# First products directly behind the first gathered rows, and a wider planning margin for routing steps in the sparse groups

## The chip, the cores and the metric

One core of a Trainium2 chip runs the whole program. The metric is the time of one execution in device microseconds (us). Other times in this document are us from the start of the profiled span unless marked ns.

## The reference

Three stages follow each other. The first is attention over a window of 64 positions (4 batches, 8 heads, 576 positions, 64 values a head). The second routes each of the 2304 resulting rows of 512 values to one of 8 experts and applies that expert's two-layer network. The third is one dense two-layer network with a squared ReLU. The routing is greedy over all scores in descending order with room for 288 rows an expert, which is what makes it a search:

```python
logits = x @ w_gate
order = np.argsort(-logits.flatten())
for idx in order:
    tok, e = idx // E, idx % E
    if assigned[tok] >= 0 or counts[e] >= cap: continue   # cap = N // E = 288
    assigned[tok] = e; counts[e] += 1
for e in range(E):
    out[assigned == e] = np.maximum(x[assigned == e] @ w1[e], 0) @ w2[e]
h = np.maximum(out @ w_in, 0)
return h * h @ w_out
```

## The kernel before

**Stages.** `attention` computes the rows and writes them to memory (`xs`) and their routing scores to `L`. Then `FFN.run` goes through the list `ORDER`: sparse groups `M` (one expert each, 288 rows) and dense groups `G` (768 rows each, the third stage): M0 M1 M2 G0 M3 M4 M5 G1 M6 M7 G2. A dense group starts as soon as the experts behind it have delivered its rows.

**The search.** An expert is filled before the next one can be chosen, so `Routing.phase(i)` finds which expert fills next and the score at which it is full. It does six rounds. Each compares all scores against a grid of thresholds on VectorE (line 392; 354 or 382 in the first round), counts on TensorE with 18 small matmuls (line 399, "count"), turns the counts into flags on VectorE (line 426), sums the flags on TensorE (line 432, "sum") and narrows the grid. A prefix sum follows (lines 469 and 470, "prefix"); it is then known which expert it is (`esi`, line 463). `Routing.slots` turns the places into row numbers with 18 more matmuls (line 516, "slots"). All of them share one bank of PSUM.

**From the search to a group.** `FFN.dispatch(i)` issues three gathers of 96 rows on GpSimd's queue (line 791), transposes them on TensorE (line 804, 12 transposes), and splits them into a high part on ScalarE (`xhi`, line 807) and the rest on VectorE (`xlo`, line 809). Each weight tile is split in the same way: the high part on ScalarE (`whi`, line 680), the rest in two halves on VectorE or GpSimd (`wlo`, line 693). A product of two such numbers takes three matmuls: high by high, high by rest, rest by high.

**A sparse group.** `FFN.M(i)` does 96 products for the first layer (8 column blocks, 4 row blocks, 3 passes; line 870) and 96 for the second (line 912), with ReLU and a split in between (lines 891 and 893). The first group, whose weights and rows arrive last, does part of its first layer differently: six column blocks are begun, two at a time, with the two passes that need only the weights' high parts (line 881, 48 products in three waves of 16), and the third pass follows later.

**What sets the order.** The program is straight-line: each engine executes its instructions in the order in which the Python code issues them. That order is made by a planner, `Clock`, which books a duration for each instruction and engine. `clk.pe` is its time; a product of a sparse group moves it by `MM_M` = 121 ns in `tick`. The search, the dispatch and the weight splits are generators. Each yields the planner's time at which it wants to go on. `route_step` resumes search and dispatch; `item_step` resumes the weight splits. `wait_until` and `run_until` take both kinds of steps until a time or a condition is reached; `idle` only moves the planner's time to the next one that something waits for and issues no step. The next weight tile of a sparse group is begun only when both rests of the tile before it have been issued. The time at which a TensorE step of the search may be issued is the planned end of the VectorE work before it plus a margin:

```python
    def after_dve(self):
        return self.dve+60+self.margin
```

The shared bank is given free at the same moment. `G` sets the margin to `MARGIN_G` at its start and to `MARGIN_M` at its end, and `run` sets `MARGIN_M` once the first search is over. Before a sparse group starts, `M` waits (in planned time) until its rows are gathered and split, and `need` waits until the weight tiles asked for are split too. `GATE` lets search 3 and later ones begin only inside dense groups.

The searches are numbered by the expert whose rows they find: search 0 has nothing beside it, searches 1 and 2 run beside the first two sparse groups.

Of the kernel before, what the change touches and what calls it, by code (L numbers as in the profile page):

```python
# [541 lines left out]
GATE_M=2  # L542
GATE=[[0, 1, 3], [0, 5, 4], [0, 9, 5], [1, 1, 6], [1, 7, 7]]
LO_EARLY=2000
MARGIN_M=100
MARGIN_G=100
MM_M=121
GATHER_0=1700
# [5 lines left out]
class FFN:  # L554
# [300 lines left out]
    def M(self, i):  # L855
        nc=self.nc
        n0=self.first["M",i]
        self.run_until(lambda: i in self.x)
        self.wait_until(self.x[i]["at"])
        self.low=n0  # L860
        self.need(n0+3,("hi",) if i==0 else ("hi","lo"))
        self.allowed=n0+8
        self.warm=None
        x=self.x.pop(i)
        h={}; ps={}; hat={}
        def mm(f, passes, c):
            for kk in range(4):
                for a,b in passes:
                    if c: self.tick(MM_M)
                    nc.tensor.matmul(ps[f][:,:CAP],self.w[n0+kk][a][:,f*128:(f+1)*128],x[b][:,kk],start=c==0,stop=c==11)  # L870
                    c+=1

        head=6 if i==0 else 0
        for f in range(0,head,2):

            for g in (f,f+1): ps[g]=self.ps.tile([128,512],F32,name="acc",bufs=6)
            for part in range(2):
                for g in (f,f+1):
                    for kk in range(4):
                        if f==0 and part==1: self.wait_until(x["lat"][kk])  # L880
                        nc.tensor.matmul(ps[g][:,:CAP],self.w[n0+kk]["hi"][:,g*128:(g+1)*128],x[("hi","lo")[part]][:,kk],start=part==0 and kk==0,stop=False)
                        self.tick(MM_M)
        if head: self.need(n0+3)
        for f in range(8):
            if f<head: mm(f,PASSES[2:],8)
            else:
                ps[f]=self.ps.tile([128,512],F32,name="acc",bufs=6)
                mm(f,PASSES,0)
            h[f]=self.htile()
            hi,lo,p=h[f]["hi"][:,:CAP],h[f]["lo"][:,:CAP],ps.pop(f)  # L890
            nc.scalar.activation(hi,p[:,:CAP],AF.Relu); t=self.clk.aop(CAP)
            def low(lo=lo,hi=hi,p=p,t=t,f=f):
                nc.vector.scalar_tensor_tensor(lo,p[:,:CAP],0.0,hi.bitcast(F32),op0=OP.max,op1=OP.subtract)
                hat[f]=self.clk.op(CAP,t,0)+60
            self.defer(t,low)
            self.tick(MM_M)
        self.l1done=i
        self.low=n0+4
        self.need(n0+7)
        self.allowed=n0+12  # L900
        s0=i*CAP
        for d in range(4):
            p=self.ps.tile([128,512],F32,name="acc",bufs=6)
            c=0

            for k,(a,b) in [(k,ab) for ab in (PASSES[0],PASSES[2],PASSES[1]) for k in range(8)] if d==0 else [(k,ab) for k in range(8) for ab in PASSES]:
                if d==0 and b=="lo":
                    self.run_until(lambda: k in hat)
                    self.wait_until(hat[k])
                o=(k%2)*512+d*128  # L910
                if c: self.tick(MM_M)
                nc.tensor.matmul(p[:,:CAP],self.w[n0+4+k//2][a][:,o:o+128],h[k][b][:,:CAP],start=c==0,stop=c==23)  # L912
                c+=1
            g0=s0//HN
            parts=[]
            for g in (g0,g0+1):
                a,b=max(s0,g*HN),min(s0+CAP,(g+1)*HN)
                if a>=b: continue
                y=self.ytile(g)
                sl=slice(a-g*HN,b-g*HN)  # L920
                parts.append((y["hi"][:,d,sl],y["lo"][:,d,sl],p[:,a-s0:b-s0],b-a))
            for yh,yl,src,n in parts:
                nc.scalar.copy(yh,src); t=self.clk.aop(n)
            def low(parts=parts,t=t):
                for yh,yl,src,n in parts:
                    nc.vector.tensor_tensor(out=yl,in0=src,in1=yh.bitcast(F32),op=OP.subtract); self.clk.op(n,t,0)
            self.defer(t,low)
            self.tick(MM_M)


    def G(self, g):
# [75 lines left out]
        self.inG=False  # L1007
        self.clk.margin=MARGIN_M
    def run(self):
        self.gens=[self.route.phase(0,self.o[0])]  # L1010
        self.run_until(lambda: not self.gens)
        self.clk.margin=MARGIN_M
        self.gens=[self.dispatch(0),self.router()]
        for kind,i in ORDER:
            getattr(self,kind)(i)
# [46 lines left out]
```

## Time and profile before

| what | us |
|---|---|
| time, median of 3 runs | 827.7 (825.53 to 828.62) |
| the profiled execution | 828.17 |
| its span | 826.5 |
| TensorE matmuls busy (PE) | 774.8, 94% of the span |
| weight loads busy (PEld) | 702.5, 85% |
| VectorE busy (DVE) | 474.4, 57% |
| ScalarE busy (ACT) | 400.5, 48% |
| GpSimd busy (POOL) | 263.9, 32% |

The profile cuts the span into 40 slices of 20.7 us. In tenths, TensorE's busy share and the clock that was granted to it are

```profile
PE   8899966899998989899999999999999999999995
PEclk9899976899998999999999999999999999999998
```

The attention stage takes the first five to six slices; search 0 stands alone behind it, and the first sparse group begins within the seventh slice. A line of the profile reads: engine, line of the kernel, operation, out<-in, tile shapes, how many. "L" is a line of the kernel printed above. PE is a matmul, PEld its weight load; SPq and POOLq are the queues on which transfers are issued. Products overlap in the pipeline, so the duration of one is longer than its spacing to the next.

### The profile page before, as it was taken

How to read it: one execution, taken by the hardware profiler on the slowest of the kernel's cores; microseconds unless marked ns; L12 is line 12 of the kernel's file. 1: busy time of each engine (PE TensorE's matmuls, PEld its weight loads, DVE VectorE, ACT ScalarE, POOL GpSimd, SP SyncE). 2: the span in 40 equal slices, each digit the busy share in tenths (PEclk: the TensorE clock that was granted, in tenths of full speed). 3: DMA queues.
4: the chain of work that ended last, by engine and by line, in shares of the span. 5: the costliest groups of instructions: out<-in, count | busy, mean ns of one | idle time of the engine just before them, and what ended most of it. 6: DMA issues, size and time to landing. Idle time of an engine off the chain costs nothing.

```text
span 826.5 us, 16334 instructions
## 1 busy us (share of the span) xinstructions
PE 774.8 (94%) x6389; PEld 702.5 (85%) x6389; DVE 474.4 (57%) x1400; ACT 400.5 (48%) x777; POOL 263.9 (32%) x240
## 2 busy tenths in 40 slices
PE   8899966899998989899999999999999999999995
PEld 7788855788997778688899998888999999999995
DVE  5687878787688999977564546542215452222111
ACT  4687722333654554643355444445445455545432
POOL 4121102333633344422254641212215462221103
PEclk9899976899998999999999999999999999999998
DMA  9999715352655565532255541223114442120001
GB/s 168 178 185 196 158 43 173 127 167 104 210 203 202 174 208 195 182 112 81 89 176 197 159 149 52 81 75 108 52 51 172 162 158 98 51 73 31 1 1 76
DMA packets 93132, 104.89 MB, mean 127 GB/s; under 512 B 59776, under 2 KB 67968, under 8 KB 93056
## 3 DMA queue, kind: packets, MB, share of 16 engines
q1 hardware_dynamic: 89984, 94.41, 39.5%
q0 software_dynamic: 3072, 9.45, 3.5%
q8 instruction: 50, 0.82, 0.4%
q14 instruction: 26, 0.21, 0.1%
HBM read 86.01 MB, written 17.84 MB: 126 GB/s over the span
## 4 chain that ended last, share of the span: by engine, by line
PE 39%; issue 15%; POOL 2%; DVE 1%; ACT 0%; POOLq 0%
PE acc L985 11%; PE l L966 11%; PE acc L870 8%; PE acc L912 7%; POOL wlo L693 2%; PE rt L399 1%; POOL out_dram L955 1%; PE acc L804 0%; PE rt L966 0%; PE rt L516 0%; PE rt L432 0%; PE rt L804 0%; DVE wt L663 0%; DVE M L456 0%; DVE hlo L975 0%
## 5 line engine op out<-in xcount | busy, mean ns | idle before, releaser
L693 POOL TENSOR_TENSOR wlo<-wr,whi 128x512 fp32r<-128x512 f32 x90 | 142.3, 1599 | 265.9 <-ACT whi L680 238.8
L975 DVE TENSOR_TENSOR hlo<-h,hhi 128x384 fp32r<-128x384 f32 x96 | 56.2, 586 | 159.0 <-ACT hhi L973 159.0
L970 ACT ACTIVATE r<-l 128x384 f32<-128x384 f32 x93 | 45.6, 490 | 191.6 <-PE l L966 191.5
L966 PE MATMUL l<-yhi,wlo 128*128 128x384 f32 x372 | 127.5, 343 | 0.0
L966 PE MATMUL l<-ylo,whi 128*128 128x384 f32 x372 | 126.6, 340 | 0.0
L966 PE MATMUL l<-yhi,whi 128*128 128x384 f32 x372 | 126.3, 340 | 0.0
L985 PE MATMUL acc<-whi,hlo 128*128 128x512 f32 x288 | 115.5, 401 | 3.8 <-DVE hlo L975 3.8
L985 PE MATMUL acc<-wlo,hhi 128*128 128x512 f32 x288 | 115.0, 399 | 0.0
L985 PE MATMUL acc<-whi,hhi 128*128 128x512 f32 x288 | 113.8, 395 | 0.0
L680 ACT CAST whi<-wr 128x1024 fp32r<-128x1024 f32 x96 | 99.8, 1050 | 28.2 <-DVE G L382 20.2
L693 DVE TENSOR_TENSOR wlo<-wr,whi 128x512 fp32r<-128x512 f32 x102 | 89.5, 883 | 22.7 <-ACT whi L680 22.5
L966 PEld LDWEIGHTS l<-yhi,whi 128*128 128x128 f32 x372 | 70.4, 189 | 4.4 <-ACT hhi L973 0.4
L870 PE MATMUL acc<-xhi,wlo 128*128 128x288 f32 x256 | 73.6, 300 | 0.0
L966 PEld LDWEIGHTS l<-ylo,whi 128*128 128x128 f32 x372 | 70.3, 189 | 3.6
L693 POOL TENSOR_TENSOR wlo<-wt,whi 128x512 fp32r<-128x512 f32 x32 | 46.8, 1485 | 81.1 <-ACT whi L680 81.1
L966 PEld LDWEIGHTS l<-yhi,wlo 128*128 128x128 f32 x372 | 70.2, 189 | 1.3 <-issue 1.1
L870 PE MATMUL acc<-xlo,whi 128*128 128x288 f32 x232 | 69.3, 299 | 0.0
L870 PE MATMUL acc<-xhi,whi 128*128 128x288 f32 x232 | 69.3, 299 | 0.0
L985 PEld LDWEIGHTS acc<-whi,hlo 128*128 128x128 f32 x288 | 54.4, 189 | 16.5 <-DVE hlo L975 4.2
L912 PE MATMUL acc<-hhi,whi 128*128 128x288 f32 x256 | 67.1, 296 | 0.0
L912 PE MATMUL acc<-hlo,whi 128*128 128x288 f32 x256 | 66.7, 296 | 0.0
L912 PE MATMUL acc<-hhi,wlo 128*128 128x288 f32 x256 | 66.4, 295 | 0.0
(198 smaller groups left out, 1473.4 us busy)
## 6 DMA issues: line engine op xcount, KB each, us to landing
wr<-in_moe_w_dram SPq DMA_DIRECT2D x32, 1024.0 KB, 5.3
wr<-conv SPq DMA_DIRECT2D x16, 1024.0 KB, 4.9
wr<-in_moe_w_in_dram SPq DMA_DIRECT2D x16, 512.0 KB, 4.5
wr<-in_moe_w_out_dram SPq DMA_DIRECT2D x16, 512.0 KB, 5.3
conv<-wt SPq DMA_DIRECT2D x16, 512.0 KB, 3.1
xs<-X SPq DMA_DIRECT2D x12, 384.0 KB, 4.6
kn<-in_k_dram SPq DMA_DIRECT2D x20, 192.0 KB, 5.1
qn<-in_q_dram SPq DMA_DIRECT2D x20, 192.0 KB, 5.4
```

Of the source, the lines that this page charges most:

```text
L399: nc.tensor.matmul(cnt[:,0:8],G[:,c],oh[:,c],start=c==0,stop=c==W-1)
L680: nc.scalar.copy(hi,src)
L693: (nc.gpsimd if p else nc.vector).tensor_tensor(out=lo[:,s],in0=src[:,s],in1=hi[:,s].bitcast(F32),op=OP.subtract)
L870: nc.tensor.matmul(ps[f][:,:CAP],self.w[n0+kk][a][:,f*128:(f+1)*128],x[b][:,kk],start=c==0,stop=c==11)
L912: nc.tensor.matmul(p[:,:CAP],self.w[n0+4+k//2][a][:,o:o+128],h[k][b][:,:CAP],start=c==0,stop=c==23)
L955: st=nc.gpsimd.indirect_dma_start(out=self.out,out_offset=bass.IndirectOffsetOnAxis(ap=idt[:,t:t+1],axis=0),in_=ot,in_offset=None)
L966: nc.tensor.matmul(p[:,:HN],self.w[n0+f][a][:,kk*128:(kk+1)*128],y[half][b][:,kk],start=c==0,stop=c==11)
L970: nc.scalar.activation(r,p[:,:HN],AF.Relu); at=self.clk.aop(HN)
L975: nc.vector.tensor_tensor(out=h["lo"],in0=h2,in1=h["hi"].bitcast(F32),op=OP.subtract); self.clk.op(HN,t,0)
L985: nc.tensor.matmul(acc[3*half+t],h[b][:,t*128:(t+1)*128],w[a][:,512:1024],start=f==0 and c==0,stop=f==15 and c==2)
```

## The change

`MARGIN_M` goes from 100 to 400 ns; `MARGIN_G` stays at 100. In `M`, the first group no longer waits in planned time for the split of its rows and for the high parts of its first four weight tiles. It only goes on with the weight splits until the four high copies have been issued. The other groups do what they did (`need` has both parts as its default).

```diff
-MARGIN_M=100
+MARGIN_M=400
 MARGIN_G=100
...
         self.run_until(lambda: i in self.x)
-        self.wait_until(self.x[i]["at"])
         self.low=n0
-        self.need(n0+3,("hi",) if i==0 else ("hi","lo"))
+        if i==0:
+
+            while not all(k in self.w for k in range(n0,n0+4)):
+                if not self.item_step(): self.idle()
+        else:
+            self.wait_until(self.x[i]["at"])
+            self.need(n0+3)
         self.allowed=n0+8
```

## Rows read from the trace of the kernel before

**Rows 1.** Stages: busy us of each engine, granted clock, DMA share, GB/s.

```profile
core 0: us, PE busy (x) PEld busy (x) DVE busy (x) ACT busy (x) POOL busy (x), PEclk, DMA share, GB/s
...
412.00:490.00 78.00, 78.00 (x600) 77.96 (x599) 42.43 (x75) 38.78 (x70) 43.15 (x32) 1.00 0.54 181
```

**Rows 2.** Chain that ended last, pieces in order of time: start, us, what.

```profile
412.07 12.79 PE acc L870 x96
```

**Rows 3.** Timeline of TensorE, 137 to 147: start, us, instruction, idle before, releaser.

```profile
137.72 0.60 PE L399 MATMUL rt<-oh,G 128*128 128x8 bf16 x18
...
141.33 0.63 PE L399 MATMUL rt<-oh,G 128*128 128x8 bf16 x18 [1.35 <-DVE G L392]
141.82 0.59 PE L881 MATMUL acc<-xhi,whi 128*128 128x288 f32 x1
...
144.83 2.12 PE L881 MATMUL acc<-xlo,whi 128*128 128x288 f32 x8
```

**Rows 4.** Timeline of ScalarE, 137 to 141.

```profile
137.72 0.40 ACT L807 CAST xhi<-acc 128x288 fp32r<-128x288 f32 x1 [3.08 <-issue]
...
138.88 2.02 ACT L680 CAST whi<-wr 128x1024 fp32r<-128x1024 f32 x2
```

**Rows 5.** Timelines of GpSimd and TensorE, 155 to 167.

```profile
155.39 4.97 POOL L693 TENSOR_TENSOR wlo<-wr,whi 128x512 fp32r<-128x512 f32 x4 [5.79 <-ACT whi L680]
...
159.22 0.19 PE L469 MATMUL rt<-M,tri 128*128 128x36 bf16 x1 [2.19 <-DVE esi L463]
160.50 0.18 PE L470 MATMUL rt<-cum,on 128*128 128x36 bf16 x1 [1.08 <-DVE cum L464]
...
165.71 1.22 PE L912 MATMUL acc<-hhi,whi 128*128 128x288 f32 x8
```

**Rows 6.** Short stages where the granted clock (PEclk) falls or returns.

```profile
141.50:142.00 0.50, 0.50 (x19) 0.50 (x15) 0.47 (x3) 0.00 (x0) 0.00 (x0) 0.50 1.36 66
...
148.00:148.50 0.50, 0.50 (x5) 0.50 (x5) 0.00 (x0) 0.00 (x0) 0.50 (x2) 0.70 1.07 410
...
162.00:163.00 1.00, 1.00 (x6) 1.00 (x5) 0.95 (x7) 0.00 (x0) 0.00 (x0) 0.50 0.84 319
...
165.00:166.00 1.00, 1.00 (x8) 1.00 (x8) 1.00 (x4) 0.09 (x1) 0.00 (x0) 0.82 1.02 422
```

**Rows 7.** Timelines of SyncE's queue and TensorE, 160 to 184.

```profile
160.31 1.07 SPq L629 DMA_DIRECT2D wr<-in_moe_w_dram  x2
...
169.39 0.61 PE L516 MATMUL rt<-Bv,A__170 128*128 128x6 f16 x18
...
180.14 0.16 PE L432 MATMUL rt<-ok,on 32*128 32x1 bf16 x1 [0.55 <-DVE ok L426]
...
183.76 0.29 PE L870 MATMUL acc<-xhi,whi 128*128 128x288 f32 x1
```

**Rows 8.** Timelines of TensorE and GpSimd, 187 to 216, and the gathers' landing there.

```profile
187.05 0.61 PE L399 MATMUL rt<-oh,G 128*128 128x8 bf16 x18 [0.30 <-DVE G L392]
...
195.68 0.61 PE L399 MATMUL rt<-oh,G 128*128 128x8 bf16 x18
...
203.59 0.61 PE L516 MATMUL rt<-Bv,A__170 128*128 128x6 f16 x18
...
207.54 1.33 POOL L791 DMA_INDIRECT xg<-xs,idx  x1 [0.30 <-issue]
DMA to landing us min/median/max: 3.5/3.9/4.6
212.04 1.16 PE L804 MATMUL acc<-identf,xg 96*128 96x96 f32 x12
...
215.56 0.29 PE L870 MATMUL acc<-xhi,whi 128*128 128x288 f32 x1
```

**Rows 9.** Waits of TensorE, 137 to 260: us in total, times, longest.

```profile
PE acc L985 <- DVE hlo L975: 3.8, 1, 3.8
PE rt L432 <- DVE ok L426: 3.6, 4, 1.5
```

## The prediction before the run

> **What bounds the kernel now.** I read the profile from the outside in: the page's slices, the stage table, then the order of TensorE's instructions inside the first three sparse groups, because both edits act there and nowhere else. In a late sparse group TensorE is busy all the time [rows 1], and 96 products follow each other in 12.79 us [rows 2], that is 0.133 us each; 192 of them, one group, cost 25.6 us. The first group does not look like that. Its first product starts at 141.82 and the second group's first one at 183.76 [rows 3, 7]: 41.9 us for 25.6 us of products. The 16.3 us between are what the change can touch, and they are search steps that stand in TensorE's order, waits for VectorE behind such steps, and a low clock. A search after the third does not stand in a sparse group: the counting matmuls of searches 3 to 7 lie in the dense groups, where the margin stays 100. So the wider margin acts on searches 1 and 2 alone.
>
> **Part 1, the first products.** Before, the planner walked on until the split of x and the four high copies of w1 were done by its clock, and put into TensorE's order what came due meanwhile: one count, one sum and a second count stand between the transposes and the first product [rows 3]. All three wait for VectorE. Now the first product comes as soon as the fourth high copy has been issued, and the loop that waits for it takes no search step. On the chip the first product then needs the first x copy, which ends at 137.72+0.40 = 138.1, and the third and fourth weight copies, which end at 139.9 and 140.9 [rows 4]. So the fourth product starts at 140.9 at the latest, and the first wave of 16 ends twelve products later: at 142.5 if they take 0.133 us, at 144.1 at the slow spacing of the present wave, 2.12/8 = 0.265 us [rows 3]. It ends at 146.95 now. Gain: 2.9 to 4.4 us.
>
> The clock decides between the two. TensorE had nearly nothing to do from 138.3 to 141.3; the granted clock was at half (1.2 GHz of 2.4) from 141.5 and came back in the slice at 148.0 [rows 6]. With products from 138.1 on the empty stretch is shorter; that it then stays up is possible, not certain, and I keep both ends.
>
> Up to product 48 the new order holds the two counts and two sums that stood ahead: 32 products, 4.3 us, and 1.1 us for the four steps, plus up to 1 us of low clock. Up to product 96 (the start of the second layer, 165.71 now [rows 5]) come 6.4 us and 1.2 us for search steps, plus 0 to 2 us of waits. What goes there is the stall of 2.19+1.08 us behind the prefix matmul and the half clock that followed it at 162 [rows 5, 6]. So the second layer starts between 155.5 and 160.1. It takes 96 products, 12.8 us, one to two more search steps, 1 us, and 0 to 1 us of waits: group 0 ends between 169.3 and 175. I take 170.5, near the early end, because the waits shrink by part 2 as well.
>
> **What is late next.** The search. Its steps have lost the head start of three steps. The counts between steps in the present order (16, 7, 10, 6, 13, 6, 11 products, then 55 to the slot matmul, which stands behind product 124 [rows 7]) average ten, so the three steps plus the sixteen products of the wave put the rest some 40 products later. Part 2 adds to that.
>
> **Part 2, the margin.** A search step goes into the order 300 ns later by the planner's clock, which counts 121 ns a product: 2.5 products more in front of each, 0.33 us of TensorE at 0.133 us. A search has 14 such steps (six counts, six sums, prefix, slots). The good side is bounded by the waits in this stretch: TensorE waited 3.6 us in four times for the flag of a count [rows 9], and the stalls above. A margin takes at most 0.33 us of each, some 2 us over both searches, already in the ranges above. The bad side: search 1 now has twelve steps behind the first product, 30 products. With the 40 from part 1 its slot matmul goes from behind product 124 to about 192: the end of the group. What stood behind it there (the first counts of search 2 and the transposes of the next x, some 5 us of the present second layer) leaves the group, and that is half of the group's gain: moved, not saved. No DMA moves by itself, but two queues follow the search: SyncE asks for expert 1's weights once the prefix step has named it (160.31 now [rows 7]), and GpSimd issues the gathers behind the slots. The weights come some 2 to 4 us later and had over 20 us to the group that reads them; for the gathers there is no such room.
>
> This rule speaks against the margin: the Trainium skill, SBUF — State Buffer, section "SBUF: two separate sides", says that VectorE (with two SBUF inputs or in a two-port mode) and GpSimd hold a shared port in turn for whole instructions. The trace bears that out: GpSimd ran four subtractions of weights, 4.97 us, over the prefix stall [rows 5]. By the rule a step that meets a subtraction waits over a microsecond, so 300 ns hides little; taking no relief from the margin would put the sum about 1 us up.
>
> **From slots to the next group.** From the slot matmul to the next group's first product runs a chain that no order shortens: index, three gathers, transposes, split. For group 2: slots 203.59, third gather issued 207.54, 3.9 us to landing (211.4), transposes 1.2 us [rows 8], first x copy 0.4 [rows 4]: 213.0, or 9.4 us after the slots; 9.0 to 10.1 by the spread of the landings. For group 1 this chain is hidden now: 169.39+9.4 = 178.8, and the group starts at 183.76 [rows 7]. With the slots at the end of group 0 it is bare: group 1 starts at 170.5+9.4 = 179.9, 3.9 us earlier than now, after some 9 us in which TensorE has only three short steps of search 2. So the clock falls there. For its price the nearest row is the fall at 162, behind 3.3 us of idling: low to about 165.4 [rows 6], 3.4 us, of which nearly half is lost, 1.5. The longer low stretch, 141.5 to 148.2, would cost 3. I take 1.5.
>
> Search 2: count, sum, count fit into the gap, the next sum (now 10.75 us after the slots [rows 7]) does not. So at the start of group 1 search 2 is a round behind. A round takes (195.68-187.05)/2 = 4.3 us [rows 8], less six products, 3.5 us. From the group's start to slots 2 it was 203.59-183.76 = 19.8; now 19.8+3.5 + ten steps at 0.33 (3.3) - 0.6 of shorter waits + 1.5 of clock = 27.5: slots 2 at 207.4, 3.8 later. The chain of 9.4 us then gives group 2 at 216.8 against 215.56 [rows 8], because its slack of 2.5 us (213.0 to 215.56) is used up first. Group 1's products end by about 212, so TensorE idles again and group 2 too begins at the low clock: another 1.5.
>
> Sum: +1.2 +1.5 = 2.7 us later at the end of group 2. The dense group behind it does not give it back: its first stall, 3.8 us [rows 9], stands behind weights that load after expert 2's, and these follow search 2. The profiled execution took 828.17 (its span 826.5, 1.7 around it), 0.5 above the median of 827.7: 830.9 beside it, 830.4 beside the median.
>
> [...]
>
> **Rivals.**
> *Slower: the search is the bound of both groups.* The point from which it decides is slots 2 at 206.1: beyond it every microsecond is the program's. For it: some 30 more products in each search and two bare gather chains. If group 0 ends at 174, at the late end, and each low clock costs 2, then group 1 starts at 183.4, slots 2 come at 211.4, group 2 at 220.8: +5.2+2 = 7, 835. Against it: a step that comes late waits for nothing, and in the gap search 2 runs undisturbed.
> *Faster: the search keeps up.* If VectorE, not the margin, sets the spacing of the steps, search 2 does not grow by 3.3; with group 0 over at 169.3 and the clock up, group 1 starts at 178.5, slots 2 come at 201.2 and group 2 starts at 210.6: -5, 823. For it: sums and counts wait up to 1.5 us for VectorE now [rows 9], time that a later place uses. Against it: 30 products a search are more than those waits.
> *The first products gain nothing*, because the fourth weight copy holds them to 140.9 and the clock falls as now. Then group 0 loses its stalls only, its slots stay inside it, and the margin makes slots 2 later by 3 to 5: 829 to 833.
>
> **How the numbers follow.** Forecast 0.42, slower 0.29, faster 0.19, no gain in front 0.10. A measurement of this kernel cannot tell less than 0.5%, 4.1 us, from no change: the borders are 823.6 and 831.8. The forecast's own range, 826 to 833, lies mostly inside; a seventh of it and half of the last case go to slower, and a few hundredths of each to faster. So faster 0.18, same 0.46, slower 0.36. The range over all cases is 822.5 (the faster case, a little past it) to 836.5 (the slower one).
>
> **What would show it.** Right: first product near 138.1 and the first wave over by 144; slots of search 1 behind product 180 to 192; an idle stretch of 5 us or more ahead of the second group and one of 3 us or more ahead of the third, each followed by half clock; the start of group 2 between 214 and 219. Wrong: the slots of search 1 well inside group 0, or group 1 and 2 starting with no gap: then the first 3 to 5 us stay won and the time is near 823.

## The result and the profile after

The changed kernel takes 835.27 us (median of 4 runs, 834.28 to 840.61) against 826.62 us (825.03 to 828.62) for the kernel before: a ratio of 1.0101, 95% interval 1.0071 to 1.0131. It is about 1% slower. The profiled execution took 835.46, 7.3 more than that of before. In `M` and behind it the changed file has five more lines: L870 is now L875, L881 is L886, L912 is L917, L966, L975 and L985 are L971, L980 and L990.

The head of the page says that no engine has much more to do; the spans differ, the busy times hardly:

```profile
span 833.4 us, 16329 instructions
PE 775.7 (93%) x6387; PEld 704.0 (84%) x6387; DVE 471.0 (57%) x1404; ACT 399.9 (48%) x777; POOL 258.1 (31%) x236
PE   8899957969998997999999999999999999999996
PEclk9999967969999999999999999999999999999998
```

TensorE is busy 0.9 us longer in a span that is 6.9 us longer: what came is mostly idle time. The medians are 8.65 us apart; the lengths below are those of the two profiled executions, 7.3 apart.

**The start of group 0**, TensorE's timeline (columns as in [rows 3]):

```profile
137.34 1.00 PE L886 MATMUL acc<-xhi,whi 128*128 128x288 f32 x3 [0.18 <-ACT xhi L807]
139.18 1.38 PE L886 MATMUL acc<-xhi,whi 128*128 128x288 f32 x5 [0.84 <-ACT whi L680]
140.36 2.12 PE L886 MATMUL acc<-xlo,whi 128*128 128x288 f32 x8
142.28 0.44 PE L886 MATMUL acc<-xhi,whi 128*128 128x288 f32 x1
```

Against [rows 3], the first product waits for the x copy and for nothing of the search, starts 4.5 us earlier, and the second wave begins at 142.28. The spacing of the third line, 2.12 us for eight, is still that of half clock; the mean granted clock was 1.00 from 137 to 139 and 0.56 from 139 to 142.3.

**From group 0 to group 1.** TensorE again; the rows answer to the prefix of [rows 5] and to the slots and first product of [rows 7]:

```profile
164.92 0.19 PE L469 MATMUL rt<-M,tri 128*128 128x36 bf16 x1
...
170.87 0.60 PE L516 MATMUL rt<-Bv,A__170 128*128 128x6 f16 x18
...
180.09 0.16 PE L432 MATMUL rt<-ok,on 32*128 32x1 bf16 x1 [2.85 <-DVE ok L426]
180.18 0.90 PE L804 MATMUL acc<-identf,xg 96*128 96x96 f32 x4
182.28 1.54 PE L804 MATMUL acc<-identf,xg 96*128 96x96 f32 x8 [1.19 <-DMA xg<-xs,idx]
183.61 0.67 PE L399 MATMUL rt<-oh,G 128*128 128x8 bf16 x18
184.14 0.59 PE L875 MATMUL acc<-xhi,whi 128*128 128x288 f32 x1
```

The prefix waits no longer. The slots of search 1 now stand behind the last product of group 0, and between 171.5 and 184.1 TensorE has only steps of search 2 and transposes, and is busy for 4.5 of these 12.6 us. Group 0 begins 4.5 us earlier, group 1 0.4 us later: nothing of the new start is left.

**From group 1 to group 2**, where [rows 8] had the slots at 203.59 and the transposes at 212.04, inside group 1:

```profile
207.59 0.61 PE L516 MATMUL rt<-Bv,A__170 128*128 128x6 f16 x18
...
215.37 0.29 PE L917 MATMUL acc<-hhi,wlo 128*128 128x288 f32 x1
215.50 1.15 PE L804 MATMUL acc<-identf,xg 96*128 96x96 f32 x12
216.90 0.40 PE L875 MATMUL acc<-xhi,whi 128*128 128x288 f32 x1 [0.24 <-ACT xhi L807]
218.70 0.40 PE L875 MATMUL acc<-xlo,whi 128*128 128x288 f32 x1 [1.40 <-DVE xlo L809]
```

The transposes now follow the last product of group 1; what they and the split take, and a wait of 1.40 us, lie bare. The first dense group begins at 244.1 instead of 241.0.

**The first dense group** ends (first product of M3) at 418.8 instead of 411.9: it is 174.7 us long and was 170.9. TensorE's waits from 240 to 420 (us in total, times, longest), first after, then before:

```profile
PE rt L432 <- DVE ok L426: 9.4, 6, 4.5
...
PE rt L399 <- DVE oh L385: 2.0, 1, 2.0
PE acc L990 <- DVE hlo L980: 1.0, 1, 1.0
...
```

```profile
PE acc L985 <- DVE hlo L975: 3.8, 1, 3.8
PE rt L432 <- DVE ok L426: 3.0, 4, 1.4
...
```

The stall of [rows 9], 3.8 us, has shrunk to 1.0. In its place the waits for the flags of the searches in this group (3 to 5) grew from 3.0 to 9.4; the longest, 4.5 at 332.28, stands behind the slots of search 3 (318.75), in the first round of search 4. The whole lists, of six rows each, add up to 15.5 and 13.5. The clock is the other part; the whole dense group and stages of it (columns as in [rows 1]), first after, then before:

```profile
244.10:418.80 174.70, 159.15 (x1090) 135.43 (x1089) 142.29 (x331) 83.74 (x136) 57.05 (x46) 0.96 0.45 153
244.10:270.00 25.90, 22.51 (x125) 19.88 (x124) 25.68 (x44) 15.63 (x26) 10.20 (x8) 0.93 0.58 198
270.00:300.00 30.00, 26.79 (x185) 22.28 (x184) 28.03 (x52) 14.63 (x23) 9.02 (x6) 0.94 0.52 181
300.00:340.00 40.00, 35.46 (x216) 31.13 (x215) 34.10 (x71) 19.10 (x31) 14.25 (x11) 0.91 0.57 189
```

```profile
241.00:411.90 170.90, 157.26 (x1090) 133.23 (x1089) 143.57 (x328) 84.10 (x136) 61.35 (x47) 0.98 0.45 154
241.00:270.00 29.00, 25.25 (x133) 22.53 (x132) 26.01 (x44) 16.48 (x27) 10.44 (x8) 0.88 0.52 177
270.00:300.00 30.00, 27.98 (x214) 23.32 (x213) 29.30 (x54) 15.53 (x24) 12.64 (x8) 1.00 0.61 207
300.00:340.00 40.00, 34.24 (x217) 28.88 (x215) 38.14 (x80) 21.47 (x34) 16.34 (x12) 1.00 0.52 176
```

VectorE is busy for 85 to 99% of these stages in both. Before, the clock fell once, behind the one stall; after, in three stages. Stage length times what the clock lacks of 1 is at most 3.5 us before and 7.2 after (25.9 x 0.07 + 30 x 0.06 + 40 x 0.09). The first rows say what came of it: with the same number of matmuls TensorE was busy 1.9 us longer (159.15 against 157.26), and so 1.9 of the 3.8 us are matmuls that took longer and 1.9 are idle time. From M3 on the changed kernel stays 6.5 to 6.9 us behind, to the end: 3.1 came in the sparse groups and 3.8 in the dense one.

### The profile page after: what moved, and what is told of

The parts are those of the page before. It is cut to its first block, busy times and chain, and to the rows that moved or that the text cites. A ratio compares the mean times of both kernels' runs of the same rounds, so it can differ in the third digit from the quotient of the medians.

```text
span 833.4 us, 16329 instructions
## 1 busy us (share of the span) xinstructions
PE 775.7 (93%) x6387; PEld 704.0 (84%) x6387; DVE 471.0 (57%) x1404; ACT 399.9 (48%) x777; POOL 258.1 (31%) x236
## 4 chain that ended last, share of the span: by engine, by line
PE 38%; issue 15%; POOL 3%; DVE 2%; DMA 1%; ACT 1%; POOLq 0%; SPq 0%; DVEq 0%; ACTq 0%
PE acc L990 11%; PE l L971 11%; PE acc L875 8%; PE acc L917 6%; POOL wlo L693 2%; PE rt L399 1%; DMA wr<-in_moe_w_out_dram 1%; POOL out_dram L960 1%; DMA wr<-conv 1%; PE acc L804 0%; DVE wt L663 0%; DVE wa L661 0%; DVE wt L665 0%; ACT wa L656 0%; PE rt L971 0%
## 5 line engine op out<-in xcount | busy, mean ns | idle before, releaser
L693 POOL TENSOR_TENSOR wlo<-wr,whi 128x512 fp32r<-128x512 f32 x86 | 138.1, 1621 | 266.4 <-ACT whi L680 243.1
L980 DVE TENSOR_TENSOR hlo<-h,hhi 128x384 fp32r<-128x384 f32 x96 | 55.6, 580 | 160.6 <-ACT hhi L978 160.3
L975 ACT ACTIVATE r<-l 128x384 f32<-128x384 f32 x93 | 45.6, 490 | 205.7 <-PE l L971 205.7
L971 PE MATMUL l<-yhi,wlo 128*128 128x384 f32 x372 | 128.0, 344 | 0.0
L971 PE MATMUL l<-ylo,whi 128*128 128x384 f32 x372 | 127.4, 342 | 0.0
L971 PE MATMUL l<-yhi,whi 128*128 128x384 f32 x372 | 127.3, 342 | 0.0
L990 PE MATMUL acc<-whi,hlo 128*128 128x512 f32 x288 | 116.1, 403 | 1.0 <-DVE hlo L980 1.0
L990 PE MATMUL acc<-wlo,hhi 128*128 128x512 f32 x288 | 115.4, 401 | 0.0
L680 ACT CAST whi<-wr 128x1024 fp32r<-128x1024 f32 x96 | 99.8, 1050 | 32.4 <-DMA wr<-in_moe_w_dram 28.2
L990 PE MATMUL acc<-whi,hhi 128*128 128x512 f32 x288 | 114.2, 396 | 0.0
L971 PEld LDWEIGHTS l<-ylo,whi 128*128 128x128 f32 x372 | 70.6, 190 | 6.2 <-issue 2.5
L971 PEld LDWEIGHTS l<-yhi,whi 128*128 128x128 f32 x372 | 70.7, 190 | 3.6
L875 PE MATMUL acc<-xhi,wlo 128*128 128x288 f32 x256 | 72.9, 298 | 0.0
L971 PEld LDWEIGHTS l<-yhi,wlo 128*128 128x128 f32 x372 | 70.8, 190 | 0.2
L990 PEld LDWEIGHTS acc<-whi,hlo 128*128 128x128 f32 x288 | 54.7, 190 | 19.2 <-issue 6.9
L875 PE MATMUL acc<-xlo,whi 128*128 128x288 f32 x232 | 69.4, 299 | 1.4 <-DVE xlo L809 1.4
L875 PE MATMUL acc<-xhi,whi 128*128 128x288 f32 x232 | 70.0, 302 | 0.2 <-ACT xhi L807 0.2
L917 PE MATMUL acc<-hhi,whi 128*128 128x288 f32 x256 | 67.5, 297 | 0.0
L917 PE MATMUL acc<-hhi,wlo 128*128 128x288 f32 x256 | 66.7, 295 | 0.0
L917 PE MATMUL acc<-hlo,whi 128*128 128x288 f32 x256 | 66.1, 295 | 0.0
```

The lines of the kernel that those rows point to most:

```text
L680: nc.scalar.copy(hi,src)
L693: (nc.gpsimd if p else nc.vector).tensor_tensor(out=lo[:,s],in0=src[:,s],in1=hi[:,s].bitcast(F32),op=OP.subtract)
L971: nc.tensor.matmul(p[:,:HN],self.w[n0+f][a][:,kk*128:(kk+1)*128],y[half][b][:,kk],start=c==0,stop=c==11)
L975: nc.scalar.activation(r,p[:,:HN],AF.Relu); at=self.clk.aop(HN)
L980: nc.vector.tensor_tensor(out=h["lo"],in0=h2,in1=h["hi"].bitcast(F32),op=OP.subtract); self.clk.op(HN,t,0)
L990: nc.tensor.matmul(acc[3*half+t],h[b][:,t*128:(t+1)*128],w[a][:,512:1024],start=f==0 and c==0,stop=f==15 and c==2)
```

## The experiments

Each was timed beside the kernel before on the same chip; they ran on three chips, so that ratios are compared and not times. Lengths are from each one's profile, in us: from the slot matmul of search 0 to that of search 1, on to that of search 2, on to group 2's first product, on to the dense group, and the length of that.

| kernel | ratio (95%) | slots 0 to 1 | 1 to 2 | to group 2 | to dense | dense |
|---|---|---|---|---|---|---|
| before | 1 | 40.4 | 34.2 | 12.0 | 25.4 | 170.9 |
| after | 1.0101 (1.0071 to 1.0131) | 42.8 | 36.7 | 9.3 | 27.2 | 174.7 |
| margin alone | 1.0095 (1.0064 to 1.0125) | 41.5 | 36.0 | 9.2 | 27.3 | 174.4 |
| new start alone | 0.9992 (0.9970 to 1.0014) | 38.4 | 34.9 | 11.7 | 25.4 | 168.4 |
| new start, search in it | 1.0043 (1.0023 to 1.0064) | 41.2 | 34.9 | 11.0 | 26.0 | 173.2 |
| after, search 3 a step later | 1.0020 (1.0003 to 1.0037) | 42.8 | 36.2 | 9.3 | 26.7 | 167.7 |
| margin 400 in search 1 | 1.0015 (0.9996 to 1.0033) | 40.9 | 34.4 | 12.8 | 25.4 | 170.2 |
| margin 400 in search 2 | 1.0067 (1.0041 to 1.0093) | 40.5 | 37.3 | 8.1 | 28.2 | 173.0 |
| new start, search 3 a step later | 0.9940 (0.9918 to 0.9962) | 39.3 | 34.7 | 11.7 | 25.4 | 164.4 |
| before, search 3 a step later | 0.9957 (0.9933 to 0.9981) | 42.4 | 34.2 | 12.0 | 25.4 | 165.3 |
| after, weights behind gathers | 1.0106 (1.0049 to 1.0164) | 43.9 | 36.6 | 9.3 | 25.9 | 171.9 |

The last row but one has before's order up to the dense group, so 40.4 against 42.4 is what one profile scatters; the ratios carry the verdicts.

**The margin alone.**

```diff
-MARGIN_M=100
+MARGIN_M=400
```

> The margin alone (400 ns, the old start). In its instruction order the slots of search 1 stand behind product 170 of the first group (124 before, 192 in the changed kernel) and those of search 2 behind product 138 of the second (114 before, 137 changed). Theory A (the margin makes the searches the bound; the new start is nearly free): group 0 ends near 180 to 183, the second group starts 3 to 5 us later than before, the third 4 to 7 later; time +5 to +8 us over before, 832 to 835. Rival S (the start alone costs, because the search loses the steps that stood ahead of the first product; the margin's steps are paid by shorter waits): within +-2.5 us of before, 824 to 829. Theory B (the first dense group's time hangs on how search steps and conversions happen to interleave): the start of that group is where A says, and its length differs from before (170.9) by 2 us or more in either direction.

Measured 835.01, 1.0095. The margin makes the whole loss.

**The new start alone** (`MARGIN_M` stays 100, `M` as in the changed kernel).

> The new start alone, with the margin at 100 ns as before. The slots of search 1 stand behind product 152, 40 short of the first group's end, those of search 2 behind product 116 of the second group. Theory A: the first product near 138, group 0 over 5 to 8 us earlier, the second group within 2 us of where it was because the gathers behind slots 1 bound it; time -2 to +2 us against before, 825 to 829. Rival S: the second and third group 3 us or more later, time +4 to +7, 831 to 834. Theory B as above: the dense group's length, not its start, carries most of any difference.

Measured 826.93, 0.9992: no difference that can be told. The first product is early here too (139.3), and search 1 ends some 2 us earlier by its profile, which is no more than one profile scatters; in the median nothing arrives.

**The new start with search steps in its loop**, margin 100, to give back the head start.

```diff
-                if not self.item_step(): self.idle()
+                x0=self.item_step(); x1=self.route_step()
+                if not (x0 or x1): self.idle()
```

> The new start with one line more: the loop that waits for the fourth high copy also takes search steps, margin 100 ns. The slots of search 1 stand behind product 126 again (124 before). If what the new start loses is the search's head start (A and S agree on that), this keeps the earlier first product and loses nothing: group 0 ends 2 to 4 us earlier than before, the second group follows it by 0 to 2 us, time -1 to -4 us, 823 to 826. If the early products only move work (the search is the bound whatever stands ahead of it), the third group starts where it did and the time is within 1.5 us of before.

A miss: 831.26, 1.0043. The steps taken in the loop stand ahead of the first product again (it starts at 143.2), slots 1 to 2 is that of the other margin-100 kernels, and the dense group, whose order of instructions comes out a third way, is 173.2 long.

**The changed kernel with search 3 let into the dense group one step later.** The sparse part is untouched.

```diff
-GATE=[[0, 1, 3], [0, 5, 4], [0, 9, 5], [1, 1, 6], [1, 7, 7]]
+GATE=[[0, 2, 3], [0, 5, 4], [0, 9, 5], [1, 1, 6], [1, 7, 7]]
```

> The changed kernel with search 3 let in one step later in the first dense group (step 2 instead of 1); nothing before that group changes, and the sparse groups' order is the same up to its start. Theory A (lateness passes through): 835 +-1.5, the dense group as long as in the changed kernel (174.7 us). Theory B (the interleaving sets it): the dense group's length moves by 2 us or more, and the time with it, to 830 to 833 or to 837 to 840, with its start unmoved.

Measured 828.89, 1.0020, under the 830 to 833 that the second reading named. Against the changed kernel's 1.0101 some 0.8% are gone, with the dense group again beginning at 243.8 and now 167.7 long. Whether this takes back what the margin cost, or would speed up any of the kernels, only the last pair below can tell. Its waits there:

```profile
PE rt L399 <- DVE oh L385: 4.1, 1, 4.1
PE rt L432 <- DVE ok L426: 2.6, 3, 1.1
...
```

The flags cost 2.6 instead of 9.4; one wait of 4.1 stands at the start of the search.

**The margin in search 1 only, and in search 2 only**, each on the kernel before (`i==1`, then `i==2`).

```diff
+            if not self.inG: self.clk.margin=400 if i==1 else MARGIN_M
             yield from self.route.phase(i,self.o[i])
```

> The old start; the margin is 400 ns for search 1 and 100 for search 2. The order of every engine inside the first dense group is then instruction for instruction that of the kernel before, while the slots of search 1 go from behind product 124 to behind product 168. Theory C (the loss is made by search 2: it is the one whose end no group hides, and its end relative to the third group decides the dense group's order): within +-2 us of before, 825.5 to 829.5; dense group 168 to 171.5 us long. Rival A (each late search passes through): half of the margin's loss, +3 to +5 us, with the second and third groups starting that much later.

> The old start; the margin is 100 ns for search 1 and 400 for search 2. The order inside the first dense group is then instruction for instruction that of the changed kernel. Theory C: nearly the whole loss, +5 to +8 us over before, 832 to 835: the dense group starts 1 to 3 us later and is 174 to 175 us long against 168.5 to 171. Rival A: +2 to +4, all of it ahead of the dense group.

Measured 828.89 (1.0015) and 832.91 (1.0067). Search 1 can be slowed for nearly nothing, because the next group has slack there: slots 1 fall back from product 124 to 168 of group 0 and group 1 hardly notices. Search 2 can't: slots 1 to 2 grows from 34.2 to 37.3, and the dense group behind it lengthens. Inside the dense group every engine has the same order of instructions in before, in the new start alone and with the margin in search 1 (170.9, 168.4, 170.2 us long); after, margin alone, margin in search 2 and the last kernel of the table share another order (174.7, 174.4, 173.0, 171.9). The longest wait in that second set is the same one. The waits with the margin in search 2 only:

```profile
PE rt L432 <- DVE ok L426: 9.5, 5, 4.5
PE rt L399 <- DVE oh L385: 2.1, 1, 2.1
```

In the changed kernel it is this piece of VectorE, GpSimd and TensorE:

```profile
326.59 5.20 DVE L404 TENSOR_SCALAR u<-hi 128x18 f32<-128x18 int32 x1
326.80 4.95 POOL L693 TENSOR_TENSOR wlo<-wt,whi 128x512 fp32r<-128x512 f32 x4
331.71 0.16 DVE L405 TENSOR_SCALAR li<-key 128x18 int32<-128x18 int32 x1
...
332.28 0.16 PE L432 MATMUL rt<-ok,on 32*128 32x1 bf16 x1 [4.54 <-DVE ok L426]
```

An instruction on 18 elements takes 5.20 us and ends with GpSimd's four weight subtractions; its twin behind it takes 0.16. Before, the same step met a series of two:

```profile
327.63 2.98 DVE L404 TENSOR_SCALAR u<-hi 128x18 f32<-128x18 int32 x1
328.05 2.52 POOL L693 TENSOR_TENSOR wlo<-wt,whi 128x512 fp32r<-128x512 f32 x2
...
331.10 0.16 PE L432 MATMUL rt<-ok,on 32*128 32x1 bf16 x1 [1.38 <-DVE ok L426]
```

This is no chance meeting: of the 1155 executions of the search's VectorE steps on 18 elements (lines 404 to 423) in the eleven traces, 90 took over 0.6 us, and every one of the 90 ended 0.03 to 0.05 us behind the end of a GpSimd subtraction. The median of the others is 0.17 us.

**The new start and the kernel before, each with search 3 a step later**, margin 100.

> The new start, margin 100, and search 3 let into the first dense group one step later. If the later entry shortens the dense group as it did in the changed kernel (167.7 against 174.7), and does so whatever stands ahead of it, this beats both kernels: -2 to -4 us against before, 823 to 825.5. If the later entry only repaired what the margin had done to that order, it is level with the new start alone: -1.5 to +1.5.

> The kernel before with search 3 let in one step later, nothing else. By the first reading above -1 to -3 us against before with a dense group of 167 to 169 us; by the second +-1.5.

Measured 823.11 (0.9940) and 824.16 (0.9957): both beat both kernels, and most of it is the later search 3. TensorE's waits in the dense group of the first of them, and its clock there:

```profile
PE rt L432 <- DVE ok L426: 4.6, 5, 1.6
...
```

```profile
241.60:270.00 28.40, 26.72 (x151) 23.86 (x151) 28.00 (x41) 18.87 (x31) 12.97 (x9) 1.00 0.63 215
...
300.00:340.00 40.00, 36.32 (x227) 30.97 (x226) 35.64 (x78) 21.94 (x34) 20.84 (x14) 1.00 0.62 212
```

No wait is over 1.6 us, and the clock is 1.00 in all stages of the group. The whole list adds up to 9.6 us, 3.9 less than before, and 3.5 of low clock are gone: 7.4, where the dense group is 6.5 shorter. The same account for the changed kernel is +2.0 of waits and +3.7 of clock, at most 5.7, where it is 3.8 longer.

This pair also answers the question left above. With the new start in both, the margin costs 1.1% while search 3 stands in its own place (1.0101 against 0.9992) and 0.8% when it comes a step later (1.0020 against 0.9940); the 0.3% between the two are within the intervals. So the later search 3 is a gain of its own, for either margin, and it doesn't show that the margin's loss hangs on where search 3 lies. In the profiles of the later search 3 the dense group is still 167.7 us long with the wide margin and 164.4 with the narrow one, although TensorE's order in it is the same in both; the wait at the first count of search 3 is 4.1 us in the one and 1.0 in the other.

**The changed kernel with expert 1's second-layer weights asked for behind the gathers**, in three rounds. In the changed kernel group 1 began 13.3 us after the slots and not the 9.4 of the forecast; the loads were issued at 175.33 and 179.75, among the gathers.

```diff
-        return kind in ("m2","c") or "esi" in self.o[i]
+        return kind in ("m2","c") or "esi" in self.o[i] and (kind=="w1" or i!=1 or self.xg1[0]>0)
...
+            i!=1 or j>0 or nc.sync.value_load(self.xg1[1].bitcast(I32)[0:1,0:1])
             nc.sync.dma_start(t.rearrange("p (k d) -> p k d",k=4), src)
```

> The changed kernel, but SyncE asks for expert 1's second-layer weights only once the third gather of expert 1's rows has landed (it reads a word of them first); the order of TensorE's instructions is as in the changed kernel. In the changed kernel the two loads were issued 4.5 and 8.9 us after search 1's slot matmuls, the third gather was issued 5.4 us after them and its rows were there 11.4 us after them, and group 1 began 13.3 us after them. Theory (the gathers share the DMA engines with these loads): the third gather lands within about 4 us, group 1 begins 10.5 to 11.5 us after the slots, and whatever search 2 can use of these 2 us comes off the time: 833 to 835, ratio 1.007 to 1.010. Rival (the gather is late for another reason, GpSimd's own work or the three gathers following each other): it still takes near 6 us, group 1 begins 13 us after the slots, and the later weights can only cost: 835 to 837.

```profile
178.14 0.91 POOL L791 DMA_INDIRECT xg<-xs,idx  x1 [0.30 <-issue]
...
181.56 0.37 SPq L632 DMA_DIRECT2D wr<-in_moe_w_dram  x1
```

The load that waits for the third gather is issued 3.4 us behind the gather's issue, where the changed kernel needed some 6 (the third gather's issue at 176.31 to the transposes at 182.28), at a DMA share of 1.02 from 178 to 180. So the loads did hold up the gathers. Group 1 begins 11.7 us after the slots (172.84 to 184.52), 1.6 earlier. It is worth nothing: 835.78, 1.0106, above the 833 to 835 expected, and slots 1 to 2 stays 36.6, because in group 1 TensorE then waits 2.0 us for search 2:

```profile
PE rt L399 <- DVE G L392: 2.0, 1, 2.0
```

## Why the prediction was right in its range and wrong in its size

**First products and group 0: right.** Forecast were the first product near 138.1, the first wave over by 142.5 to 144.1, slots 1 at about product 192 and the end of group 0 at 170.5. They came at 137.3, 142.5 (140.36+2.12), 192 and 170.9. Two of the four are right in part by luck. The wave reached the early end of its range, which stood for the full clock, at half clock: the fourth product did not wait until 140.9, it began at 139.18. And slots 1 came to 192 by a head start of 28 products and not 40 (124 to 152 with the new start alone) and a margin of 40 and not 30 (152 to 192). That the gain moves out of the group instead of being kept was right as well; the new start alone has a ratio of 0.9992.

**The chain to group 1: mis-sized, without effect.** Forecast 9.4 us, measured 13.3. The landings of [rows 8] did not stand for these. The experiment on the weights shows both that they caused part of it and that the time didn't hang on it: search 2 did.

The other part stands on VectorE. Timelines of VectorE and GpSimd between the slots and group 1:

```profile
177.10 2.67 DVE L411 SCALAR_TENSOR_TENSOR yf<-Rs,u 128x18 f32<-128x18 f32 x1
...
177.23 2.50 POOL L693 TENSOR_TENSOR wlo<-wr,whi 128x512 fp32r<-128x512 f32 x2
```

A search step of 18 elements lasts until the two subtractions are over; the sum behind it waited 2.85 us. The Trainium skill, SBUF — State Buffer, section "SBUF: two separate sides", says that a VectorE step with two SBUF inputs, as this one has, and a GpSimd operation that reads SBUF get a shared port for whole instructions, whichever starts first, while the other is blocked. The trace agrees that VectorE is blocked for whole instructions of GpSimd, 2.67 us here. It does not show that the first to start goes first: this step starts 0.13 us ahead of two subtractions and ends behind both, and the one of 5.20 us in the dense group starts 0.21 us ahead of four. Which condition of the rule the 5.20 us step met, with its one input, no run here shows.

**Slots 2 and group 2: right in time, partly for other reasons.** Slots 2 were forecast at 207.4 and came at 207.6; group 2 at 216.8 and 216.9. But the terms differed. Group 1 began 4.2 us later than forecast, and search 2 took 23.5 us from there and not 27.5; the two errors cancel because search 2 goes on in the gap (36.7 us from slots 1 to slots 2, forecast 36.9). The prediction had TensorE idle for 3 us or more ahead of group 2; it was busy until 215.5, so that this sign of being right did not come. It was the transposes that moved from inside group 1 to its end. The 1.5 us put down for a low clock at group 2 were 1.40 us of waiting for the split at full clock. The clock, over the start of group 1 and over that of group 2:

```profile
185.00:190.00 5.00, 5.00 (x45) 4.64 (x44) 3.74 (x12) 2.68 (x5) 2.96 (x2) 0.78 0.04 14
215.50:220.00 4.50, 2.85 (x24) 2.46 (x23) 4.24 (x8) 2.04 (x7) 1.19 (x1) 1.00 0.85 242
```

At group 1 it did fall, as forecast: the mean over 185 to 190 was 0.78. The Trainium skill, TensorE: Matmul & The Clock Gate, section "HAM oscillation — how this bites in real kernels", tells of a kernel in which every burst of matmuls begins throttled behind a DMA wait of some 3 to 5 us. Group 1 agrees with it, behind 12.6 us in which TensorE was busy for 4.5; the 1.40 us at group 2, with the clock at 2.4 GHz behind them, are shorter than that kernel's waits and do not test it. The clock is no constant of this place either: with the margin in search 2 only, waits of 0.91 and 1.13 us there, and one of 0.61 for the gather ahead of them, go with a mean of 0.62 over 215 to 219.

The end of the sparse part came 3.1 us late, against a sum of 2.7.

**The step that failed: "The dense group behind it does not give it back".** The reason given was that its first stall stands behind weights that follow search 2. In fact that stall nearly vanished, 3.8 to 1.0, which alone would have given 2.8 us back. And then the group lost more than that again. The prediction treated it as a block of fixed length that shifts, though its order is made by the same planner, from the state that search 2 leaves: the steps of searches 3 to 5 came to stand among other weight splits, on a VectorE that is busy for some nine tenths of the time up to 340. That term, 174.7-170.9 = 3.8 us, was put at nothing; 3.1+3.8 = 6.9, and 0.4 outside the profiled span (835.46-833.4 = 2.1 around it, 1.7 before) make the 7.3. Its size is that of one pair of profiles: kernels with the order of before took 168.4 to 170.9 us, those with the new one 171.9 to 174.7.

**The rivals.** *Slower: the search is the bound of both groups* named 835, the time that came, but that is a coincidence, for its conditions did not hold: group 0 was to end at 174 and slots 2 to come at 211.4 (170.9 and 207.6). Of its reason one half holds: search 2 sets the pace. From its slots 1 to its slots 2 it took 34.2 to 34.9 us in every kernel with margin 100 in search 2 and 36.0 to 37.3 in every one with 400; in the mean this is 2.0 us, for a forecast of 3.3. *Faster: the search keeps up* fell by the same numbers. *The first products gain nothing* fell by the timeline.

**What stays open.** That the loss is the margin's, and for the most part that of search 2, is shown by the runs with the margin alone (1.0095) and in one search (1.0067 against 1.0015). That the dense group becomes longer behind it is seen in each pair of profiles with the same start and the same place of search 3 (168.4 to 174.7, 170.9 to 174.4, 164.4 to 167.7); why it does so is not shown. The new order goes with it, but with search 3 a step later the group is longer by 3.3 us in one and the same order of TensorE. That search steps are held up by GpSimd's subtractions is shown by the 90 long steps; that this makes up the 3.8 us is read from the traces, the 5.20 us step above all. No run took these subtractions off GpSimd.

## What to carry to other kernels

Where one planner writes the order of the whole program, a change of a planning constant moves the order far behind the place where it acts: compare the lengths of all later stages before explaining the stage that was edited, and give the first of them a term of its own in the sum. A step that is planned later waits less, but it is also later; where the result gates the next stage, here search 2, that is paid (0.7%), and where slack follows, here search 1, it costs nearly nothing (0.15%, not clear of no change). When an edit far down seems to undo a loss, make the same edit on the kernel without the loss before calling it the cause. When a gain vanishes between two stages, look for the chain that both share (here the search) before freeing the transfer that seems late.

## What was not expected of the hardware

Three gathers of 96 rows, which land in 3.0 to 4.6 us before, needed about 6 us for the last of them beside 1 MB weight loads from SyncE's queue, at a DMA share of 0.98 to 1.02; with the loads held back it was 3.4. VectorE instructions on 18 elements took 0.16 us alone and up to 5.20 us beside a series of four GpSimd subtractions of weights (4.95 us), though they started 0.21 us ahead of it.
